# Groups 3 to 5 of a decayed-attention and SwiGLU kernel take the row-pair layout (NAT0 from 3 to 6)

## The chip, the core and the metric

The kernel runs on one core of one Trainium2 chip. The metric is the device time of one execution in microseconds (us). Five engines take part: TensorE (PE, matrix multiplies), VectorE (DVE), ScalarE (ACT), GpSimd (POOL) and SyncE (SP, which here only issues transfers). Each engine works through its own list of instructions in order and waits at an instruction until the data, the buffer and the bank it needs are there. Transfers (DMAs) are issued by SP and by ACT and run on 16 shared DMA engines.

## The reference

Inputs are q, k and v of shape 4 batches x 8 heads x 768 rows x 64, one decay `lam` a head (0.97 to 0.99), and three weight matrices. Attention goes over blocks of 64 rows and carries a 64x64 state a head:

```python
intra = np.einsum('bhic,bhjc->bhij', qb, kb) * Dmask[None]     # lam ** (i - j) below the diagonal
intra = np.einsum('bhij,bhjd->bhid', intra, vb)
inter = np.einsum('bhid,bhde->bhie', qb * lam_pow[None], kv_state)
out[:, :, sl] = intra + inter
kv_state = lam_block * kv_state + np.einsum('bhsd,bhse->bhde', kb_dec, vb)
```

The result, as a matrix x of 3072 x 512, goes through a gated block: `(silu(x @ w_gate) * (x @ w_val)) @ w_out`, with an inner width of 1536. Everything is float32 outside; the kernel computes in bf16 with float32 sums.

## The kernel before

**Tiling.** The rows are cut into 12 groups: a group is 256 rows of one batch, all 8 heads. Groups 0 to 3 are the first 256 rows of batches 0 to 3, groups 4 to 7 the second 256, groups 8 to 11 the last. Two groups make one tile of 512 tokens for the gated block, so there are six tiles, t = 0 to 5. All the work is written out by hand in one order: `steps` lists the gated block's 12 column steps of each tile (`ffn_fc`, lines 516 to 535), and `plan` hangs other work after chosen steps (`at(...)`, lines 669 to 748). The scheduling of the framework is manual: on each engine instructions stand in the order in which they are written.

**A group's path.** `load_group` (L244) issues its loads on SP. `cast_scaled` (L258, groups 3 and up) casts k to bf16 on ACT (L261), multiplies q by the decay on DVE (L263), then calls `dma_transpose` (L251), which puts one transposing DMA on SP (L254), and then `load_group(g + 2)`: SP issues the loads of the group after next behind the transpose. `v_scale` (L236) multiplies v by the decay on POOL. On PE come `upd_mm` (L386, products k x v for the state), `scores` (k x q), `inter` (L469, state x q) and `intra` (L482, masked scores x v). The scores are masked on DVE from PSUM into `ssb`; the copies of `upd_mm`'s result out of PSUM (`ups`, L410) and the casts of the outcome (`evac`, L494) are ACT's, in a few places DVE's; `state` (L416) adds up the state on POOL.

**Two layouts.** `NAT0` (L56) says how many groups take the first one.

- g < NAT0, the row-pair layout: a partition holds two adjacent rows of a head. One DMA loads all of k (or q, or v) of a group (L99), in pieces of 512 bytes. The group is handled as two halves of 128 rows. `scores` issues 32 products of 64x128 into four banks and defers four masks of 128x512 (L330, L337); `intra` is 32 products of 64x128; `inter` is 8 (first group of a batch) or 16 products of 64x128. `state` adds two parts.
- g >= NAT0, the plain layout: a partition holds rows p and p + 128, and half of the partitions hold the heads in reverse. k and q of a group take four DMAs each, v two (L106), in pieces of 256 bytes. The group is handled as four quarters of 64 rows. `scores_n` (L344) issues 32 products of 64x64 into two banks and defers two masks (L356, L361); `intra` is 32 products of 64x64; `inter` is 24 or 32 of 64x64; `state` adds four parts and casts three partial states in between (L427, L436, L438).

Masks are deferred in the list `later`; `run_later` works off one or two of them after each step. `attend(g)` (L558) holds `inter` of g, the update of g + 1, the scores of g + 1 and `intra` of g; for g + 1 >= NAT0 the scores stand before `intra`, else behind it (L564, L568).

**What orders the work around the change.** SP's list from the output weights on is, before: six loads of output weights (L228), ten loads of group 3, ten of group 4, the transpose of group 3, ten loads of group 5, the transpose of group 4, ten of group 6, the transpose of group 5, ten of group 7, the transpose of group 6, and so on. All DMAs of SP and ACT share eight completion semaphores in turn, and each waits until the one before it on its semaphore has landed. PSUM is used as a ring of eight banks (`bank`, L79): `ring` counts up and each new result takes the next one.

PE's order there is: the last steps of tile 0, the first half of tile 1 (s1a), `ffn_out` of tile 0 (three blocks of 12 products of 128x512, L546), `ahead(3)` (update, state and scores of group 3), the fourth block, s1a steps 9 and 10, `core(3)`, step 11, the second half s1b with `ahead(4)` after its step 5, `ffn_out(1, 0)`, `attend(4)`, three more blocks of `ffn_out`, `attend(5)`, and from there tile 2.

Of the kernel before, what the change touches and what calls it, by code (L numbers as in the profile page):

```python
# [14 lines left out]
def bap(t: bass.AP, ap_dims, extra_offset=0) -> bass.AP:  # L15
    return bass.AP(tensor=t.tensor, offset=t.offset + extra_offset,
                   ap=[list(t.ap[0])] + [list(d) for d in ap_dims])


@with_exitstack  # L20
def kernel(
    ctx: ExitStack,
    tc: tile.TileContext,
    q: bass.AP,
    k: bass.AP,
    v: bass.AP,
    lam: bass.AP,
    moe_w_gate: bass.AP,
    moe_w_val: bass.AP,
    moe_w_out: bass.AP,  # L30
    out: bass.AP,
):
    nc = tc.nc
    with tc.manual_schedule():
        _body(ctx, tc, nc, q, k, v, lam, moe_w_gate, moe_w_val, moe_w_out, out)


def _body(ctx, tc, nc, q, k, v, lam, moe_w_gate, moe_w_val, moe_w_out, out):
# [14 lines left out]

    NAT0 = 3  # L56
    NB = 4
    PB = B // 2
    groups = [(t % PB * 2 + j, t // PB) for t in range(NG // 2) for j in range(2)]
# [25 lines left out]
    def gsrc(t, g, h0):  # L85
        b, i = groups[g]
        return bass.AP(tensor=t.tensor,
                       offset=t.offset + b * H * S * D + i * 2 * BLK * D + h0 * S * D,
                       ap=[[2 * D, 2 * M], [S * D, H - h0], [1, 2 * D]])
# [3 lines left out]
    def load_fp32(g, eng, src, what, h0=0, h1=H):  # L93
# [3 lines left out]
        t = st[(what, g)]  # L97
        if g < NAT0:
            eng.dma_start(out=t[:, h0:h1], in_=gsrc(src, g, h0)[:, 0:h1 - h0])  # L99
# [87 lines left out]
    def vfac(g, h0, h1):  # L187
        return bap(dec, [[8, h1 - h0], [1, 2], [0, D]], 8 * h0 + (0 if g < NAT0 else 4))

    def qfac(g):  # L190
        return bap(dec, [[8, H], [1, 2], [0, D]], 2) if g < NAT0 else bap(qdn, [[2, H], [1, 2], [0, D]])

# [119 lines left out]
    def scores(g, cs=(0, 1), warm=0):  # L312
        if g >= NAT0:
            scores_n(g)
            return
        tt = st[("qkt", g)]
        sp = {(c, h2): bank() for c in cs for h2 in range(2)}
        warm_into(sp[(cs[0], 0)], warm)
        if ("ssb", g) not in st:
            st[("ssb", g)] = ssb_pool.tile([128, 2, HP, 2, BLK], BF16, name="ssb", tag="ssb")  # L320
        ssb = st[("ssb", g)]
        for c in cs:
            for hi in range(2):
                for s in range(2):
                    for b2 in range(2):
                        for h2 in range(2):
                            hp = 2 * c + hi
                            dp = slice(h2 * 64, h2 * 64 + 64)
                            n = (hi * 2 + s) * BLK
                            nc.tensor.matmul(  # L330
                                sp[(c, h2)][b2 * M:b2 * M + M, n:n + BLK],
                                tt[dp, 0, s, hp, b2 * M:b2 * M + M],
                                tt[dp, 1, :, hp, b2 * M:b2 * M + M],
                                start=True, stop=True, skip_group_check=True)
            for h2 in range(2):
                def do_mask(c=c, h2=h2):
                    nc.vector.tensor_tensor(  # L337
                        out=ssb[:, h2, 2 * c:2 * c + 2].rearrange("p a s n -> p a (s n)"),
                        in0=sp[(c, h2)].rearrange("p (a x) -> p a x", a=2),
                        in1=bap(causal, [[0, 2], [1, 2 * BLK]]),  # L340
                        op=ALU.mult)
                later.append(do_mask)

    def scores_n(g):  # L344
        tt = st[("qkt", g)]
        sp = [bank() for _ in range(2)]
        ssb = ssb_pool.tile([128, 2, HP, 2, BLK], BF16, name="ssb", tag="ssb").rearrange(
            "p a h s n -> p (a h s n)")[:, 0:2 * BLK * H // 2].rearrange("p (a h n) -> p a h n", a=2, h=H)
        st[("ssb", g)] = ssb
        for hp in range(HP):  # L350
            for s in range(2):
                for h2 in range(2):
                    for r in range(2):
                        row, hq = (1 - h2, HP - 1 - hp) if r else (h2, hp)
                        dp, rm = slice(row * 64, row * 64 + 64), slice(r * M, r * M + M)
                        nc.tensor.matmul(sp[h2][rm, (hp * 2 + s) * M:(hp * 2 + s) * M + M],  # L356
                                         tt[dp, 0, s, hq, rm], tt[dp, 1, s, hq, rm],
                                         start=True, stop=True, skip_group_check=True)
        for h2 in range(2):
            def do_mask(h2=h2):  # L360
                nc.vector.tensor_tensor(out=ssb[:, h2], in0=sp[h2].rearrange("p (a x) -> p a x", x=M),  # L361
                                        in1=bap(causaln, [[0, 2 * HP], [1, M]]), op=ALU.mult)
            later.append(do_mask)
# [6 lines left out]
    def upd_mm(g, up=None):  # L370
# [4 lines left out]
        for s in range(2):  # L375
            for hp in range(HP):
                for r in range(2):
                    if g >= NAT0 and i == NG // B - 1 and 2 * s + r == 3:
                        continue
                    for h2 in range(2):  # L380
                        ps = slice(r * M, r * M + M)
                        h = 2 * hp + h2
                        if g >= NAT0 and r:
                            h = H - 1 - h
# [405 lines left out]
```

## Time and profile before

| what | value |
|---|---|
| median of 3 runs | 245.96 us (245.46 to 246.36) |
| the profiled execution's own time | 246.36 us |
| its span, first to last instruction | 244.6 us |
| mean granted PE clock | 0.965 of full |
| PE busy | 223.0 us, 91% |
| ACT, POOL, DVE busy | 108.4, 95.4, 88.1 us |
| the chain that ended last | PE 76%, DMA 13%, POOL 6% |
| SP's queue (q1) | 93026 packets, 32.65 MB |
| packets under 512 bytes, of all | 76418 of 97565 |

PE's own work fills nine tenths of the span, so this kernel is PE's length plus PE's pauses. The chain says who stretches it beyond that: 13% of the chain is DMA. The shares of busy time of the other engines (36 to 44%) say nothing of a bound. The lines to look for are those in which PE stands idle, and the granted clock behind each of them.

### The profile page before, as it was taken

The page shows a single profiled execution, that of the slowest core. Times are in us where ns is not written, and L with a number is a line of the kernel's source. Part 1 is how long each engine was busy: PE and PEld are TensorE (multiplying, and loading weights), DVE is VectorE, ACT ScalarE, POOL GpSimd, SP SyncE. Part 2 cuts the span into 40 slices and gives each one's busy share as a digit, 9 for nine tenths or more (in the row PEclk, how much of TensorE's full clock was granted, in tenths as well). Part 3 has the DMA queues.
Part 4 walks back from the last instruction along what each step waited for, and adds up shares of the span by engine and source line. Part 5 has one row for each costly group of instructions (what it writes and reads, how often), then busy time and mean ns, then how long its engine had stood idle before and what let it go on. Part 6 is the DMA issues. An engine that isn't in the chain of part 4 may idle for free.

```text
span 244.6 us, 6085 instructions
## 1 busy us (share of the span) xinstructions
PE 223.0 (91%) x2497; PEld 122.3 (50%) x2508; DVE 88.1 (36%) x151; ACT 108.4 (44%) x211; POOL 95.4 (39%) x146
## 2 busy tenths in 40 slices
PE   7999998993499979379999999999999999999994
PEld 3665456841258844165545445454454444444443
DVE  3663356420316640035564426235324222242200
ACT  5876764734026543224646327235362352222211
POOL 5566647333700778770495607409124000000000
PEclk9999999999579999958999999999999999999999
DMA  7999999699896957977888874410510111001122
GB/s 210 345 362 372 360 351 354 144 240 251 182 244 156 219 138 181 200 168 179 181 183 192 191 182 120 129 46 3 129 46 3 43 46 43 30 15 43 43 86 86
DMA packets 97565, 39.71 MB, mean 162 GB/s; under 512 B 76418, under 2 KB 93058, under 8 KB 97538
## 3 DMA queue, kind: packets, MB, share of 16 engines
q1 hardware_dynamic: 93026, 32.65, 53.5%
q10 hardware_dynamic: 4512, 6.69, 7.5%
q8 instruction: 19, 0.31, 0.5%
q14 instruction: 8, 0.07, 0.1%
HBM read 28.31 MB, written 6.29 MB: 141 GB/s over the span
## 4 chain that ended last, share of the span: by engine, by line
PE 76%; DMA 13%; POOL 6%; ACT 1%; issue 1%; DVE 1%; SPq 0%; POOLq 0%; DVEq 0%; ACTq 0%
PE bank L546 24%; PE bank L524 22%; PE bank L531 21%; DMA qkt<-qk 7%; DMA wraw<-in_moe_w_val_dram 3%; DMA v<-in_v_dram 3%; PE bank L482 2%; POOL v_s L239 2%; POOL kvf L427 1%; PE bank L386 1%; PE bank L469 1%; PE bank L356 1%; PE bank L168 1%; PE bank L293 1%; POOL kvs L430 1%
## 5 line engine op out<-in xcount | busy, mean ns | idle before, releaser
L534 DVE TENSOR_TENSOR h<-sil,bank 128x512 bf16<-128x512 bf16 (+1 forms) x89 | 51.9, 585 | 103.8 <-PE bank L531 87.4
L524 PE MATMUL bank<-xt,wg_sb 128*128 128x512 bf16 (+1 forms) x356 | 78.6, 344 | 0.0
L531 PE MATMUL bank<-xt,wv_sb 128*128 128x512 bf16 (+1 forms) x356 | 78.2, 343 | 0.0
L528 ACT ACTIVATE sil<-bank 128x512 bf16<-128x512 f32 (+1 forms) x89 | 46.1, 520 | 47.6 <-PE bank L524 43.8
L546 PE MATMUL bank<-wo_sb,h 128*128 128x512 bf16 (+1 forms) x289 | 66.3, 380 | 0.7 <-issue 0.2
L531 PEld LDWEIGHTS <-wv_sb 128*128 128x128 bf16 x356 | 35.5, 100 | 28.1
L524 PEld LDWEIGHTS <-wg_sb 128*128 128x128 bf16 x356 | 34.2, 100 | 27.4 <-issue 0.5
L546 PEld LDWEIGHTS <-h 128*128 128x128 bf16 x300 | 29.7, 100 | 33.8 <-issue 2.7
L548 ACT COPY osb<-bank 128x512 f32<-128x512 f32 (+1 forms) x24 | 13.9, 577 | 62.8 <-PE bank L546 62.8
L427 POOL TENSOR_TENSOR kvf<-kvs,ups 128x256 f32<-128x256 f32 x8 | 5.8, 726 | 57.4 <-ACT ups L410 54.7
L239 POOL TENSOR_TENSOR v_s<-v,dec 128x1024 bf16<-128x1024 f32 (+1 forms) x14 | 23.5, 1683 | 9.9 <-DMA v<-in_v_dram 9.7
L361 DVE TENSOR_TENSOR ssb<-bank,causaln 128x512 bf16<-128x512 f32 x18 | 12.2, 687 | 32.7 <-PE bank L356 32.6
L436 POOL CAST kvn<-kvf 64x256 bf16<-64x256 f32 x34 | 16.6, 487 | 2.1
L427 POOL TENSOR_TENSOR kvf<-kvf,ups 128x256 f32<-128x256 f32 x22 | 16.8, 764 | 1.1
L356 PE MATMUL bank<-qkt 64*64 64x64 bf16 x288 | 4.9, 206 | 12.2 <-DMA qkt<-qk 12.2
L494 ACT CAST xt<-bank 128x512 bf16<-128x512 f32 x21 | 12.1, 632 | 7.3 <-PE bank L482 6.9
L410 ACT COPY ups<-bank 128x512 f32<-128x512 f32 (+1 forms) x24 | 10.8, 503 | 3.0 <-PE bank L386 2.1
L263 DVE TENSOR_TENSOR qk<-qraw,qdn 128x1024 bf16<-128x1024 f32 x9 | 11.1, 1230 | 0.3 <-DMA qraw<-in_q_dram 0.3
L356 PEld LDWEIGHTS <-qkt 64*64 64x64 bf16 x288 | 3.9, 114 | 12.4 <-DMA qkt<-qk 12.4
L261 ACT CAST qk<-kraw 128x1024 bf16<-128x1024 f32 x9 | 9.4, 1039 | 0.0
L222 POOL CAST wv_sb<-wraw 128x1024 bf16<-128x1024 f32 (+1 forms) x7 | 6.4, 920 | 6.9 <-DMA wraw<-in_moe_w_val_dram 6.8
L337 DVE TENSOR_TENSOR ssb<-bank,causal 128x512 bf16<-128x512 f32 x12 | 7.9, 682 | 1.6 <-PE bank L330 1.6
(61 smaller groups left out, 116.2 us busy)
## 6 DMA issues: line engine op xcount, KB each, us to landing
out_dram<-osb ACTq DMA_DIRECT2D x23, 256.0 KB, 2.4
v<-in_v_dram SPq DMA_DIRECT2D x22, 256.0 KB, 4.2
kraw<-in_k_dram SPq DMA_DIRECT2D x36, 128.0 KB, 3.1
qraw<-in_q_dram SPq DMA_DIRECT2D x36, 128.0 KB, 3.2
woraw<-in_moe_w_out_dram SPq DMA_DIRECT2D x6, 512.0 KB, 9.3
wraw<-in_moe_w_gate_dram SPq DMA_DIRECT2D x5, 512.0 KB, 7.3
wraw<-in_moe_w_val_dram SPq DMA_DIRECT2D x5, 512.0 KB, 6.9
kraw<-in_k_dram SPq DMA_DIRECT2D x4, 256.0 KB, 4.4
```

The lines of the kernel that those rows point to most:

```text
L239: eng.tensor_tensor(out=st[("vs", g)][:, h0:h1], in0=st[("v", g)][:, h0:h1].rearrange("p h (s d) -> p h s d", s=2), in1=vfac(g, h0, h1), o ...
L356: nc.tensor.matmul(sp[h2][rm, (hp * 2 + s) * M:(hp * 2 + s) * M + M], tt[dp, 0, s, hq, rm], tt[dp, 1, s, hq, rm], start=True, stop=True, s ...
L361: nc.vector.tensor_tensor(out=ssb[:, h2], in0=sp[h2].rearrange("p (a x) -> p a x", x=M), in1=bap(causaln, [[0, 2 * HP], [1, M]]), op=ALU.mult)
L427: nc.gpsimd.tensor_tensor(out=o, in0=f, in1=u, op=ALU.add)
L436: nc.gpsimd.tensor_copy(out=o[64 - h2 * 64:128 - h2 * 64], in_=f[h2 * 64:h2 * 64 + 64])
L494: fns[r](out=xt[:, g % 2, :, r].rearrange("p h (m s) -> p h s m", s=2) if g < NAT0 else xt[:, g % 2, :, :, r * M:r * M + M], in_=op[r].rea ...
L524: nc.tensor.matmul(gp[:, 0:N], wg_sb[:, mc, fs], xt[:, b0 // 2:b1 // 2, mc].rearrange("p g b n -> p g (b n)"), start=(mc == 0), stop=(mc = ...
L528: nc.scalar.activation(sil[:, 0:N], gp[:, 0:N], AF.Silu)
L531: nc.tensor.matmul(vp[:, 0:N], wv_sb[:, mc, fs], xt[:, b0 // 2:b1 // 2, mc].rearrange("p g b n -> p g (b n)"), start=(mc == 0), stop=(mc = ...
L534: nc.vector.tensor_tensor(out=h_sb[:, fc, b0:b1].rearrange("p b n -> p (b n)"), in0=sil[:, 0:N], in1=vp[:, 0:N], op=ALU.mult)
L546: nc.tensor.matmul(ps, h_sb[:, fc, b], wo_sb[:, fc, c0:c1], start=(fc == 0), stop=(fc == FC - 1))
L548: fn(out=osb[:, c0:c1], in_=ps)
```

## The change

One constant is changed:

```diff
-    NAT0 = 3
+    NAT0 = 6
```

Groups 3, 4 and 5 then take the row-pair layout wherever the code asks `g < NAT0` or `g >= NAT0`. They keep `cast_scaled` with its transposing DMA. On the engines' lists this does the following.

- SP: the ten loads of each of groups 3, 4 and 5 become three (k, q, v whole, L99), 512-byte pieces in place of 256-byte ones. The order of loads and transposes stays; the loads of groups 6 and up stay ten.
- PE: `scores` (L330) in place of `scores_n` (L356) for groups 3 to 5; products of 64x128 in place of 64x64 in `intra` and `inter`, with 8 in place of 24 in `inter` of group 3 and 16 in place of 32 in groups 4 and 5. In `attend(4)` the scores of group 5 now stand behind `intra` of group 4.
- DVE: four masks (L337) in place of two (L361) for each of the three groups. L263 reads its factor from `dec` in place of `qdn`.
- ACT: `ups` copies of 256 columns in place of 512; for group 3 one cast more (`kvn`, L402).
- POOL: for group 3 one add, one multiply and one cast in place of three adds, five casts, one multiply and one cast; for groups 4 and 5 two adds, one cast of a partial state, one multiply and one cast in place of four adds, five casts of partial states, one multiply and one cast.
- PSUM: `scores` takes four banks of the ring in place of two, so that the banks that follow shift by two for each of the three groups.
- The eight DMA semaphores are dealt out anew, since there are fewer DMAs.

## The prediction

> **What bounds the kernel now.** I read the page's chain first: PE 76%, DMA 13%, POOL 6%. So the end is set by PE and by what PE waits for. Next came the waits of PE between 38 and 106 us, which add up to nearly all of its idle time behind 38 us; from 110 us to the end the same view shows 0.3 us of waits. Each row gives what was waited for: us in total, times, longest.
>
> ```profile
> PE bank L356 <- DMA qkt<-qk: 12.2, 2, 7.0
> PE bank L386 <- POOL v_s L239: 1.8, 2, 1.6
> ```
>
> The reader is to see two long waits for a transposed group (qkt) and one for a scaled v. PE's timeline puts them in place (start, duration, instruction, idle time before it):
>
> ```profile
> 56.92 0.45 PE L386 MATMUL bank<-v_s,qk 64*64 64x64 bf16 x32
> 64.39 0.64 PE L356 MATMUL bank<-qkt 64*64 64x64 bf16 x32 [7.03 <-DMA qkt<-qk]
> 90.02 0.45 PE L386 MATMUL bank<-v_s,qk 64*64 64x64 bf16 x32 [1.55 <-POOL v_s L239]
> 105.20 0.64 PE L356 MATMUL bank<-qkt 64*64 64x64 bf16 x32 [5.16 <-DMA qkt<-qk]
> ```
>
> These are the scores of group 3, the update of group 5 and the scores of group 6. Behind the two long pauses PE is slow as well. The stages (window, length, busy us of PE, PEld, DVE, ACT, POOL, then the granted clock, DMA share, GB/s):
>
> ```profile
> 64.40:70.30 5.90, 5.68 (x45) 2.48 (x47) 2.42 (x3) 0.00 (x0) 1.95 (x2) 0.50 0.87 197
> 88.40:90.10 1.70, 0.15 (x19) 0.08 (x12) 0.00 (x0) 0.47 (x2) 1.57 (x1) 1.00 0.59 185
> 105.20:111.30 6.10, 6.10 (x88) 4.56 (x89) 2.13 (x4) 2.35 (x6) 3.71 (x5) 0.50 0.72 162
> ```
>
> After 7.03 and 5.16 us of idleness the clock was 0.50 for about 6 us; after 1.55 us it stayed 1.00. Last, why the transposes are late: SP's timeline.
>
> ```profile
> 48.47 3.35 SPq L106 DMA_DIRECT2D kraw<-in_k_dram  x4
> 51.92 3.31 SPq L106 DMA_DIRECT2D qraw<-in_q_dram  x4
> 55.46 1.41 SPq L106 DMA_DIRECT2D v<-in_v_dram  x2
> 57.06 4.49 SPq L254 DMA_TRANSPOSE qkt<-qk  x1
> ...
> 90.75 3.13 SPq L106 DMA_DIRECT2D qraw<-in_q_dram  x4
> 93.98 1.19 SPq L106 DMA_DIRECT2D v<-in_v_dram  x2
> 95.34 4.82 SPq L254 DMA_TRANSPOSE qkt<-qk  x1
> ```
>
> DVE finished the cast of group 3 at 51.28 (50.06 + 1.22), but SP was issuing loads of group 4 until 56.87, so the transpose left at 57.06 and landed 7.3 us later. Group 6 is alike: cast done at 87.17, transpose at 95.34, behind the ten loads of group 7, landing 9.8 us later. **The bound between 57 and 111 us is SP's list of issues**, 10 loads a group at some 0.63 us each.
>
> **What goes.**
>
> - First pause: 7.03. Its slow clock: the scores took 0.64 where group 4's took 0.40 (79.69 to 80.09), and twelve products of L546 took 65.03 to 70.27 = 5.24 where later blocks of twelve take 2.59. That is 0.24 + 2.65 = 2.9.
> - The wait for v_s of group 5: 1.55.
> - Second pause: 5.16. Its slow clock: 105.20 to 111.30 holds scores, intra and six groups of four 256-column products, at full clock 0.40 + 0.37 + 6 x 0.44 = 3.4, so 2.7.
> - Sum 19.3 us.
>
> **First pause, step by step.** In the new list SP has six issues for groups 3 and 4 in place of twenty. The new form's rows are the loads of group 2 (1.23, 2.54 and 0.69 us of issue). Six times 0.7 to 2.5 from 35.33 gives 40 to 50; the wait on the weight transfers ahead of them (their semaphores come round again, the last seen at about 45) is inside that. So SP is free before the cast ends at 51.0 to 51.3, and the transpose leaves then. It lands in 3.8 (fastest row, nothing beside it) to 7.3 us: 55 to 58.5, and PE asks at 57.36. I take no pause; at the upper end 1.1 us are left, short enough to keep the clock by the 1.55 row.
>
> Bytes could still hold it: groups 3 and 4 are 3.1 MB behind the output weights. From 6 to 9 us, where k, q and v of the first groups ran in 512-byte pieces, the DMA view shows 345 GB/s; a stretch of 256-byte pieces, 72 to 73 us, shows 290. At 345 the backlog that starts at about 44 is gone by 53, and the transpose lands by 57.
>
> **A rule against it.** The Trainium skill, DMA: Bandwidth & Descriptors, section "Issuing engines are not separate DMA queues", says that the time a sequencer takes to start a DMA is usually small beside the DMA itself. By that rule fewer issues would buy next to nothing and the sum would be a loss of about 2 us. The rows agree for a single load (0.63 against 3.1 to landing), but twenty in one line held back a transpose for 5.8 us.
>
> **Wait for v_s of group 5.** POOL ran the state of group 4 from 80.63 to 88.06, then v_s for 1.91. Two adds at 0.72, a cast at 0.40, a multiply at 0.61 and a cast at 0.40 make 2.9 in place of 7.4: 4.5 earlier covers 1.55. This goes.
>
> **Second pause.** Everything behind 57.4 moves 9.9 us earlier, and asks earlier too, by 1.55 more; so the transpose of group 6 has to gain on PE. SP, new: transpose 4 when its q is cast, at about 61.3 (scores at 57.4, three masks of 0.69, one cast of 1.22; free since some 58). It holds SP to 63 or 64.4 (1.6 to 3.1 in the rows). Ten loads of group 6 at 0.63 take it to 70 or 71. Transpose 5, whose cast is done at 68.9, leaves at 70.8 and holds SP to 74.2. Ten loads of group 7 take it to 80.6. In the old run two loads between 82 and 112 us waited 6.3 us in all for an output transfer with the same semaphore (87.14 to 90.75, among group 7's, is the larger part); in the new list no load of group 7 follows an output on its semaphore that isn't long done. Transpose 6 leaves at 80.7 and lands 5.5 to 9.8 later: 86.2 to 90.5.
>
> PE asks for it at: 57.4 + (88.47 - 64.39 = 24.1) - 2.9 + 1.2 (below) = 79.8 for the end of inter of group 4; update and intra 0.9; scores of group 5 0.6; three output blocks 7.8 and 0.3 (below); inter and update 0.8: about 90.2. So it lands at the latest as it is asked for. The same holds on the way: transpose 4 lands by 67.4, asked at 70.2; transpose 5 by 77.5, asked at 80.7. **I take the second pause as gone**, with 1.0 us left here or at the scores of group 7, whose transpose comes behind the loads of group 8.
>
> **What comes.**
>
> - PE: scores 34.44 to 35.01 against 0.40 (+0.17), intra 39.68 to 40.26 against 72.80 to 73.17 (+0.21). Inter of 16 x 64x128 isn't in the trace; between 8 of them (0.41) and 32 of 64x64 (about 0.43 to 0.5), I take no change. Three groups: 1.1.
> - DVE: six masks of 0.68, 4.1 us. Behind scores 3 an output block (2.59) and behind scores 5 three of them cover. Behind scores 4 there are only steps of 0.87, and the ring comes round after four allocations to the score banks: with masks and h products in turn, masks 3 and 4 end at about 3.4 and 4.4 us from the scores' start, where PE asks at 3.2 and 3.7. Cost 0.75; if masks are early 0, if all four are waited for 2.7.
> - ffn_out(1, 1) takes the first bank of group 4's outcome, which ACT casts last: 0.3.
> - The factor of L263 read from `dec`: not in the trace; between the plain DVE cast (0.42 for half, 0.85) and POOL's product with `dec` (1.91), near its own row, 1.22. Off the path either way.
> - Fewer copies on ACT and POOL: off the path, nothing.
>
> Sum: 19.3 - 1.1 - 0.75 - 0.3 - 1.0 = 16.2. The profiled execution took 246.36 (span 244.6 and 1.76 around it), so 230.2; it stands 0.4 above the median, so **229.8 us**.
>
> **Rivals.**
>
> A. The second pause stays. The transpose of group 6 still stands behind ten loads in the old form, and one landed in 9.8. If each such load takes 0.84 (as group 4's ten did, 48.47 to 56.87 with their gaps) instead of 0.63, transpose 6 leaves at 85 and lands at 95: 5 us of pause and the 2.7 of clock come back in place of the 1.0: 229.8 + 6.7 = 236.5. Whether a smaller rest costs the clock isn't in the trace between 1.55 and 5.16. Chance 0.20. (The skill, TensorE: Matmul & The Clock Gate, section "What's actually happening", puts the fall at about 3.4 us of idleness; by it a rest of under 3.4 stays without the 2.7.)
>
> B. The first pause only shrinks, since the transposes themselves are slow under load (7.3), and the weight casts or the loads come later by a few us: half of the first pause and all of the second: 239 to 243. Chance 0.06.
>
> C. Slower. The pacing goes: six large loads stand in front of transpose 3 in the DMA queues instead of in SP's list. If these pieces moved at the 225 GB/s that the stretch 47 to 57 shows, 3.1 MB from 44 would end at 58, the transpose would land where it did, 64.4, and each later one likewise; the added PE work and mask waits (2.1) would remain: 248. It decides from about 240 GB/s downward. Against it stand the 345. Chance 0.06.
>
> No measurable change (within 0.3%, 0.7 us, about what a measurement here can tell from none): 0.02.
>
> Forecast 0.66. Low end: all 19.3 and half of the added PE work, 227; high end rival A, 237. **Faster 0.92, same 0.02, slower 0.06.**
>
> **What would show it.** Right: SP's transpose of group 3 at 51 to 52, no wait over 1.5 us at L330 at about 57, clock 1.00 from 57 to 80, POOL's state of group 4 about 3 us long, scores of group 6 at 90 to 92. Wrong: a wait for qkt at the scores of group 3 (B, C), a pause over 3 us at group 6's (A), DVE late by more than 1 us behind scores 4.

## The result and the profile after

| | before | after |
|---|---|---|
| median of 4 runs | 245.71 us (242.93 to 246.36) | 232.24 us (231.17 to 234.25) |
| the profiled execution | 246.36 us, span 244.6 | 234.25 us, span 232.5 |
| granted clock, mean | 0.965 | 1.000 |

The ratio is 0.948, with a 95% interval of 0.938 to 0.959: 13.5 us less, where 16.2 were forecast (229.8 us, range 227 to 237). A few executions of the kernels below run slow as a whole at a lower granted clock (one of e6 at 286.77 us, one of e10 at 243.69), and the ratios leave them out.

PE's waits from 38 us to the end, after the change (total us, times, longest):

```profile
PE bank L356 <- DMA qkt<-qk: 3.6, 2, 2.9
PE bank L330 <- DMA qkt<-qk: 1.3, 1, 1.3
PE bank L482 <- ACT guard L451: 1.2, 4, 0.4
```

Where 12.2 us were spent waiting for transposes, 4.9 are left, and POOL's v_s is no longer in the list. PE's timeline tells which they are:

```profile
57.86 0.64 PE L330 MATMUL bank<-qkt 64*64 64x128 bf16 x32 [1.32 <-DMA qkt<-qk]
...
75.47 0.60 PE L531 MATMUL bank<-xt,wv_sb 128*128 128x256 bf16 x4 [0.33 <-DVE ssb L337]
...
83.12 7.93 PE L546 MATMUL bank<-wo_sb,h 128*128 128x512 bf16 x35 [0.39 <-ACT xt L494]
...
92.61 0.45 PE L356 MATMUL bank<-qkt 64*64 64x64 bf16 x32 [0.74 <-DMA qkt<-qk]
...
106.03 0.45 PE L356 MATMUL bank<-qkt 64*64 64x64 bf16 x32 [2.87 <-DMA qkt<-qk]
```

The scores of group 3 wait 1.32 in place of 7.03, those of group 6 0.74 in place of 5.16, and a new pause of 2.87 stands at the scores of group 7. Behind scores 4 one wait of 0.33 for a mask is listed, and `ffn_out(1, 1)` waits 0.39 for its bank. The stages behind the first two (the columns are those of the prediction's stages, the clock stands behind the five engines):

```profile
57.80:63.50 5.70, 5.37 (x67) 3.39 (x69) 5.18 (x6) 2.76 (x7) 3.61 (x4) 1.00 1.00 322
92.60:97.10 4.50, 4.49 (x96) 3.85 (x97) 2.62 (x6) 3.66 (x8) 3.80 (x8) 1.00 0.58 151
```

Where the clock was 0.50 it is 1.00 now. SP's timeline:

```profile
43.23 2.15 SPq L99 DMA_DIRECT2D kraw<-in_k_dram  x1
45.47 1.35 SPq L99 DMA_DIRECT2D qraw<-in_q_dram  x1
46.87 1.44 SPq L99 DMA_DIRECT2D v<-in_v_dram  x1
51.53 3.19 SPq L254 DMA_TRANSPOSE qkt<-qk  x1
...
84.71 3.67 SPq L254 DMA_TRANSPOSE qkt<-qk  x1
88.42 7.04 SPq L106 DMA_DIRECT2D kraw<-in_k_dram  x4
95.51 2.67 SPq L106 DMA_DIRECT2D qraw<-in_q_dram  x4
98.28 1.20 SPq L106 DMA_DIRECT2D v<-in_v_dram  x2
99.64 4.21 SPq L254 DMA_TRANSPOSE qkt<-qk  x1
```

Group 4's loads end at 48.31 in place of 56.87, and the transpose of group 3 leaves when its cast is done. The one of group 6 leaves at 84.71 in place of 95.34. Behind it the loads of group 8 are still in the old form, and the transpose of group 7 stands behind them. SP's waits put 3.3 us of the 7.04 for group 8's k down to an output transfer that had the same completion semaphore.

### The profile page after: what moved, and what is told of

Same layout as the page of the kernel before. It is cut to its first block, busy times and chain, and to the rows that moved or that the text cites. A ratio compares the mean times of both kernels' runs of the same rounds, so it can differ in the third digit from the quotient of the medians.

```text
span 232.5 us, 5937 instructions
## 1 busy us (share of the span) xinstructions
PE 219.2 (94%) x2449; PEld 120.5 (52%) x2460; DVE 95.4 (41%) x157; ACT 108.0 (46%) x212; POOL 84.9 (36%) x127
## 4 chain that ended last, share of the span: by engine, by line
PE 81%; DMA 11%; DVE 3%; SPq 1%; ACT 1%; issue 1%; ACTq 0%; DVEq 0%
PE bank L524 26%; PE bank L531 26%; PE bank L546 22%; DMA qkt<-qk 9%; PE bank L482 2%; DMA qraw<-in_q_dram 2%; DVE ssb L337 2%; PE bank L469 1%; SPq L99 1%; PE bank L330 1%; PE bank L356 1%; PE bank L386 1%; PE bank L293 1%; DVE h L534 0%; PE bank L168 0%
## 5 line engine op out<-in xcount | busy, mean ns | idle before, releaser
L524 PE MATMUL bank<-xt,wg_sb 128*128 128x512 bf16 (+1 forms) x356 | 77.0, 339 | 0.0
L546 PE MATMUL bank<-wo_sb,h 128*128 128x512 bf16 (+1 forms) x289 | 63.9, 370 | 1.0 <-ACT xt L494 0.4
L548 ACT COPY osb<-bank 128x512 f32<-128x512 f32 (+1 forms) x24 | 13.9, 577 | 55.8 <-PE bank L546 55.8
L337 DVE TENSOR_TENSOR ssb<-bank,causal 128x512 bf16<-128x512 f32 x24 | 15.6, 683 | 11.7 <-PE bank L330 11.6
L361 DVE TENSOR_TENSOR ssb<-bank,causaln 128x512 bf16<-128x512 f32 x12 | 8.2, 687 | 12.2 <-PE bank L356 12.0
L436 POOL CAST kvn<-kvf 64x256 bf16<-64x256 f32 x24 | 12.5, 521 | 1.5
L427 POOL TENSOR_TENSOR kvf<-kvf,ups 128x256 f32<-128x256 f32 x16 | 11.6, 725 | 0.6
L410 ACT COPY ups<-bank 128x256 f32<-128x256 f32 (+1 forms) x24 | 9.5, 449 | 1.1 <-PE bank L386 0.7
L482 PE MATMUL bank<-ssb,v_s 64*64 64x128 bf16 (+1 forms) x384 | 7.3, 207 | 1.7 <-ACT guard L451 1.2
L263 DVE TENSOR_TENSOR qk<-qraw,qdn 128x1024 bf16<-128x1024 f32 x6 | 8.6, 1432 | 0.0
L482 PEld LDWEIGHTS <-v_s 64*64 64x64 bf16 x384 | 5.8, 105 | 3.0 <-issue 3.0
```

The costliest lines, as they stand in the source:

```text
L337: nc.vector.tensor_tensor(out=ssb[:, h2, 2 * c:2 * c + 2].rearrange("p a s n -> p a (s n)"), in0=sp[(c, h2)].rearrange("p (a x) -> p a x", ...
L427: nc.gpsimd.tensor_tensor(out=o, in0=f, in1=u, op=ALU.add)
L436: nc.gpsimd.tensor_copy(out=o[64 - h2 * 64:128 - h2 * 64], in_=f[h2 * 64:h2 * 64 + 64])
L482: nc.tensor.matmul(op[r][h2 * 64:h2 * 64 + 64, cols(g, hp, s)], v_s[ps, 2 * hp + h2, s], ssb[ps, h2, hp * 2 + s] if g >= NAT0 else ssb[ps, ...
L524: nc.tensor.matmul(gp[:, 0:N], wg_sb[:, mc, fs], xt[:, b0 // 2:b1 // 2, mc].rearrange("p g b n -> p g (b n)"), start=(mc == 0), stop=(mc = ...
L546: nc.tensor.matmul(ps, h_sb[:, fc, b], wo_sb[:, fc, c0:c1], start=(fc == 0), stop=(fc == FC - 1))
```

## The experiments

Three theories stood against each other. S: SP's list ahead of each transpose was shortened, by fewer issues. B: the larger pieces move faster. P: the rest of the layout does it, POOL's shorter state above all. Edits add lines, so a line number in a view can differ from the one named before by a few. Medians below are beside the kernel before on the same chip: 244.27 us for e1 to e5, 244.79 for c0, e9, e7 and e6, 244.14 for e10 and e11.

**e1: ten issues again, 512-byte pieces.**

```diff
-            eng.dma_start(out=t[:, h0:h1], in_=gsrc(src, g, h0)[:, 0:h1 - h0])
+            n = (h1 - h0) if g < 3 else 4 if what == "v" else 2
+            for a in range(h0, h1, n):
+                eng.dma_start(out=t[:, a:a + n], in_=gsrc(src, g, a)[:, 0:n])
```

> The changed kernel (NAT0 = 6) with the loads of groups 3 to 5 cut by heads into ten issues a group again, still in 512-byte pieces; nothing else differs. Theory S (SP's list of issues is what was shortened): the transpose of group 3 leaves behind twenty issues again, at 55 to 57 us in place of 51.5, both long pauses of PE come back with the half clock behind them, and the time is 241 to 247. Theory B (the larger pieces make the transfers faster): the pieces are those of the changed kernel, so 231 to 235. Theory P (the shorter chain of states on POOL, and the layout otherwise): likewise 231 to 235.

Measured: 233.86 us, ratio 0.957 (0.951 to 0.963). S, which had 241 to 247, fails in this form; B and P had 231 to 235. SP's timeline for group 4 and the transpose of group 3 shows why:

```profile
44.97 1.99 SPq L101 DMA_DIRECT2D kraw<-in_k_dram  x4
47.06 1.96 SPq L101 DMA_DIRECT2D qraw<-in_q_dram  x4
49.06 1.02 SPq L101 DMA_DIRECT2D v<-in_v_dram  x2
50.83 3.51 SPq L256 DMA_TRANSPOSE qkt<-qk  x1
```

The same ten issues take 5.1 us (44.97 to 50.08) in place of 8.4: as long as the three of the changed kernel (43.23 to 48.31). The transpose leaves early, but it lands some 9 us later: the scores of group 3 start at 59.81, behind a pause of 3.23. Why it lands so late is open.

**e2: the transpose of group 3 amid the loads of group 4.**

```diff
-    at(s0[7], load_group, 4)
+    at(s0[7], load_group, 4, "k")
...
         dma_transpose(g)
+        if g == 3:
+            load_group(4, "qv")
```

> The kernel before, layout and loads as they were, with the transpose of group 3 moved up in SP's list: it stands behind the four k loads of group 4 and ahead of group 4's q and v loads. Theory S: the transpose leaves at about 52 in place of 57.06 and the first pause of PE shrinks from 7.03 us to under 1.5. The list is no shorter, so each later transpose gains only what the first did: 52 + 38 (as from 57.06 to 95.34) puts that of group 6 at 90, and pauses of 3 to 6 us in all come back at the scores of groups 4 to 6; 237 to 242. Theories B and P: nothing that they name is changed, 244 to 247.

Measured: 240.80 us, ratio 0.987 (0.982 to 0.993), inside S's range and under that of B and P. The transpose left at 50.82 and the first pause went. PE's timeline shows where it came back:

```profile
73.36 0.45 PE L358 MATMUL bank<-qkt 64*64 64x64 bf16 x32 [2.25 <-DMA qkt<-qk]
84.77 0.44 PE L358 MATMUL bank<-qkt 64*64 64x64 bf16 x32 [0.66 <-DMA qkt<-qk]
100.42 0.64 PE L358 MATMUL bank<-qkt 64*64 64x64 bf16 x32 [6.35 <-DMA qkt<-qk]
```

The pauses add up to 9.3 us, where S had 3 to 6. So SP's list is the bound over several groups: an earlier place helps one transpose, and only a shorter list helps those behind it.

**e3: plain layout, three issues of 256-byte pieces.**

```diff
+        if g < 6:
+            eng.dma_start(out=t.rearrange("p h (s d) -> p (h s) d", s=2),
+                          in_=bass.AP(tensor=src.tensor, offset=base,
+                                      ap=[[D, 128], [S * D // 2, 2 * H], [1, D]]))
+            return
```

> The kernel before, plain layout with all its work on PE, DVE, ACT and POOL, where k, q and v of groups 3 to 5 are each loaded by one issue of 2048 pieces of 256 bytes. The rows that arrive are not the right ones for half of the partitions and columns, so the output is not the reference's; the amount of data and of work is the same. Theory S: ten issues a group become three, the first pause goes and the second goes or shrinks to under 3 us, 231 to 236 (the wait of 1.55 for v_s may stay, the added PE work of the other layout is not there). Theory B: pieces of 256 bytes as before, 244 to 247. Theory P: POOL's chain as before, 244 to 247. If one issue of 2048 pieces holds SP as long as four of 512, S fails in its form and the number of pieces would be the bound: 244 to 247 with issues of some 2.5 us each.

Measured: 235.06 us, ratio 0.961 (0.956 to 0.967). That is S's range (231 to 236) and not that of B and P (244 to 247): without larger pieces, fewer issues bring most of the gain too. SP's timeline:

```profile
45.06 2.19 SPq L104 DMA_DIRECT2D kraw<-in_k_dram  x1
47.35 2.51 SPq L104 DMA_DIRECT2D qraw<-in_q_dram  x1
49.91 2.32 SPq L104 DMA_DIRECT2D v<-in_v_dram  x1
52.41 4.61 SPq L259 DMA_TRANSPOSE qkt<-qk  x1
```

And PE's:

```profile
59.29 0.45 PE L361 MATMUL bank<-qkt 64*64 64x64 bf16 x32 [2.60 <-DMA qkt<-qk]
...
95.96 0.44 PE L361 MATMUL bank<-qkt 64*64 64x64 bf16 x32 [2.19 <-DMA qkt<-qk]
```

Each issue of 2048 small pieces holds SP for 2.2 to 2.5 us, 7.2 for the group: little shorter than ten (8.4). Over groups 3 and 4 together the list falls from 21.5 us (35.33 to 56.87) to 18.0 (34.23 to 52.23). The pauses are down to 2.60 and 2.19. The second has a cause of its own: the list ahead of the transpose of group 6 was done at 84.37, but the transpose left at 90.23, and SP's waits put 5.7 us of this down to an output transfer with the same semaphore. Behind the first pause the clock still fell, to 0.50 from 60.6 to 63.8; behind the second it stayed. The fall shows in twelve products of 128x512, beside those of e1, whose pause was longer:

```profile
60.38 2.76 PE L548 MATMUL bank<-wo_sb,h 128*128 128x512 bf16 x12
```

```profile
59.67 4.45 PE L551 MATMUL bank<-wo_sb,h 128*128 128x512 bf16 x12
```

The first row is e1's, behind 3.23 us of pause, the second e3's, behind 2.60. So 1.7 of the 2.9 us that the prediction put behind the first pause is still paid here, and the 2.7 behind the second is not.

**e5: NAT0 = 9.** The edit is the constant alone.

> NAT0 = 9: groups 6 to 8 take the row-pair layout too. Theory S: in the changed kernel the next pause is that of 2.9 us at the scores of group 7, whose transpose stands behind ten loads of group 8 (four of them took 7.04 us); with three loads a group for 6 to 8 it leaves as soon as its cast is done, that pause and the 0.74 at group 6 go, against 3 x 0.4 us more of PE work and some waits for masks: 229 to 232. Theory P expects a gain from POOL's shorter states, which nothing waits for there: no change from 232, or 1 us more for the PE work.

Measured: 233.04 us, ratio 0.954 (0.950 to 0.958): no better than NAT0 = 6, and above S's 229 to 232. No wait for a transpose is left; what PE waits for is the row-pair layout's own:

```profile
PE bank L482 <- ACT guard L451: 1.7, 5, 0.5
PE bank L524 <- ACT xt L494: 1.2, 3, 0.4
PE bank L531 <- DVE ssb L337: 0.7, 2, 0.3
```

With the larger products (0.4 a group by the prediction's estimate) this takes back about what the pauses had cost.

**e9: plain layout, ten issues of 512-byte pieces.** The edit is e1's, in the branch of the plain layout, for g < 6.

> The kernel before, plain layout with all its work on the engines, ten issues a group for groups 3 to 5 as before, but each in 512-byte pieces (by heads, the row-pair source). The rows land in the wrong places for the plain layout, so the output is not the reference's; data and work are the same in amount. Theory S2, formed after the run with ten issues in the changed layout: SP is held by what the DMA engines and the queue take for the pieces, 8.4 us for a group in ten issues of 256-byte pieces, 5.1 in ten of 512-byte pieces, 7.1 in three of 256-byte pieces. By it the transpose of group 3 leaves within 1 us of its cast, the first pause is under 4 us and keeps the clock, and the time is 232 to 237. Theory P (POOL's chain and the layout made the gain in that run): 243 to 247. Theory S in its first form (the count of issues): 243 to 247.

Measured: 233.82 us, ratio 0.959 (0.951 to 0.967). Count of issues, products, masks and POOL's chain are as before. The pieces changed, and with them an issue of k or q reaches 128 partitions in place of 64, which isn't separated. All but some 1.5 us of the gain is there, and the intervals overlap. So the gain doesn't need P, nor the smaller count of S; the second form, S2, holds. The list of groups 3 and 4 takes 15.5 us here (34.23 to 49.73).

**c0: the changed kernel again.**

> The changed kernel as it is, beside the three that follow: all theories 231 to 233.5. Its profile tells whether the pause of 2.9 us at the scores of group 7 and the long casts of q (2.52 and 2.97 in place of 1.22 us) come again.

Measured: 232.26 us. In its profile (span 229.8) the casts of q take 1.25 and 1.45, the transpose of group 3 leaves at 50.64, nothing waits at its scores, and the scores of group 7 wait 1.76.

**e7: v of group 3 scaled on DVE** (`v_scale, 3, nc.vector`).

> The changed kernel with v of group 3 scaled on DVE, behind the cast of q of group 3, in place of POOL. Theory L (the cast of q and POOL's scaling, both reading two or one operands from SBUF, shut each other out; the cast waited for POOL's instruction of 1.91 us to end): the cast of group 3 takes 1.22 us in place of 2.52, the transpose of group 3 leaves about 1.3 us earlier, the pause of 1.32 at the scores of group 3 goes, the cast of group 4 stays long (2.9) beside POOL's scaling of group 4; 230 to 232. Rival (the cast is slower because its factor is read from the other table, with a wider step): the cast of group 3 stays at 2.5 and nothing is gained, 231.5 to 233.5.

Measured: 233.11 us against c0's 232.26: no gain. The cast of group 3 took 1.22, as theory L says, with the same table; but c0 had no pause there to win. In its profile the clock fell to 0.50 behind a pause of 1.95 at the scores of group 7, where c0's stayed at full behind 1.76.

**e6: v loads one transpose later.**

```diff
         dma_transpose(g)
-        load_group(g + 2)
+        if g < 4:
+            load_group(g + 2)
+        else:
+            if g > 4:
+                load_group(g + 1, "v")
+            load_group(g + 2, "kq")
```

> The changed kernel with the v loads of groups 6 and up issued one transpose later: behind the transpose of the group before theirs, so that only eight loads stand ahead of each transpose from that of group 5 on. Theory S2: 1.2 us less of SP's list and 0.5 MB less in the queues ahead of each transpose; the transpose of group 7 is issued when its cast ends, the pause of 2.9 us at the scores of group 7 falls to under 1.5, and that of 0.74 at group 6 goes: 229.5 to 232. Rival (that pause comes from loads of k that wait for an output transfer with the same semaphore, whatever the length of the list): no change, 231.5 to 233.5.

Measured: 229.41 us, ratio 0.940 (0.933 to 0.948), against c0's 232.26 beside it: the fastest kernel of the study, a tenth of a microsecond under S2's range. PE's waits from 38 us on hold no transpose any more:

```profile
PE bank L487 <- ACT guard L456: 1.4, 5, 0.5
PE bank L551 <- ACT xt L499: 0.4, 1, 0.4
PE bank L536 <- DVE ssb L342: 0.3, 1, 0.3
```

The transpose of group 7 left at 96.11, when its cast was done (95.97); in the changed kernel it left 1.6 us after its cast, in c0 1.2. That is S2's forecast. The rival isn't ruled out by it: a new order deals the semaphores anew, and SP's waits for output transfers among the loads of that stretch fell too, from 3.3 us in the changed kernel and 3.9 in c0 to 2.4.

**e10 and e11: the same move of v with NAT0 = 3 and with NAT0 = 5.**

> The kernel before (NAT0 = 3, 256-byte pieces), its only edit that v of each group from 4 on is loaded one transpose later, so that eight loads stand ahead of each transpose in place of ten. Theory S2: the transpose of group 3 leaves about 1.5 us earlier (55.5 on the old run's clock, 54 to 55 where the start is a little faster), which leaves 3.5 to 5 us of the first pause, and each group's list is 1.2 us shorter: the one of group 6 leaves about 5 us earlier. 236 to 242. If the layout is needed for the gain: 243 to 246.

> NAT0 = 5 with v loaded one transpose later (from group 6 on, as in the fastest kernel so far with NAT0 = 6): group 5 goes back to the plain layout, with ten loads of 256-byte pieces, two masks less and smaller products. Theory S2: eight fewer pieces' worth of list matter little there, since the transpose of group 5 had 2 to 4 us to spare; 0.4 us less of PE work, 228.5 to 231. Rival (each group that stays with 256-byte pieces costs a third of the gain of 13 us): 232 to 235.

Measured: e10 237.33 us, ratio 0.972 (0.968 to 0.977), pauses of 2.62 and 2.52 left, with the clock at 0.50 for some 3.5 us behind both; the move alone gives half of the change's gain. Its list ended at 53.00 and the cast of group 3 at 50.36, but the transpose left at 55.41: SP's waits put 2.3 us down to an output transfer with the same semaphore. e11 231.07 us, ratio 0.947 (0.943 to 0.951), at the edge of S2's range and under the rival's; its transpose of group 6 left at 86.32, where e6's left at 80.65. Its cast was done at 77.65 and its list at 82.93; here SP waited 3.2 us for an output transfer.

So beside the length of the list there is a second thing that holds a transpose back: the output transfer that happens to have its semaphore (5.7 us in e3, 2.3 in e10, 3.2 in e11). No run changes the semaphores alone.

## Why the prediction was right, and where it wasn't

- **Right: which waits go.** Both long pauses, the slow clock behind them and the wait for v_s went. The transpose of group 3 left at 51.53 (forecast 51.0 to 51.3). That this time fits is luck: the cast started 1.2 us earlier than before (48.85 against 50.06) and took 1.3 longer. POOL's state of group 4 took 3.0 us, 71.89 to 74.91 (2.9).
- **Right in kind, wrong in its reason: "SP's list of issues, 10 loads a group at some 0.63 us each".** That SP's list is the bound stands by e2 and e10, and e6 agrees. That the count of issues alone makes its length doesn't: for group 4, ten issues of 512-byte pieces take 5.1 us, ten of 256-byte pieces 8.4, three of 256-byte pieces 7.2, three of 512-byte pieces 5.1. For groups 3 and 4 together it is 21.5 before, 18.0 with fewer issues alone (e3), 15.5 with larger pieces alone (e9) and 13.9 with both (34.43 to 48.31). The size of the pieces moved the list more than the count did, and either alone is enough for most of the gain. Whether the DMA engines or the making of the pieces' descriptors sets these times isn't separated here. A hint: from 46 to 48 us the DMA share was 0.84 before (189 GB/s), 1.12 in e3 (254 GB/s) and 0.98 in e9 (275 GB/s).
- **The rule that was set against the change** said that the number of issues counts for little. Between 512-byte forms that is so: e1's ten against three is 233.86 against 232.24, with intervals that overlap. With 256-byte pieces it isn't: e3's three against ten is 235.06 against 244.27. The prediction set the rule aside for a reason that covers half of the case. The Trainium skill, DMA: Bandwidth & Descriptors, section "Specifications", gives 512 bytes as the least transfer for full rate; e9 is the run that shows what that is worth here.
- **"The factor of L263 ... near its own row, 1.22. Off the path either way" failed.** In the profiled execution the casts of groups 3 and 4 took 2.52 and 2.97. This made the transpose of group 4 leave at 63.24 (forecast 61.3). At group 3 it is the likely cause of the 1.32 that is left of the first pause, since a cast of 1.22 would have let the transpose go 1.3 earlier; no run shows it, as e7 had no pause there to win.
- **Mis-sized: the 1.0 for a rest at group 6 or 7.** It measured 0.74 + 2.87 in the profiled execution, 1.76 in c0. The 2.87 kept the clock by luck: behind 1.94 (e11) and 1.95 (e7) at the same place it fell. Group 6's transpose left at 84.71, not 80.7: 1.9 from the cast of group 4, the rest from a transpose that held SP 4.14 and loads of group 7 that took 7.6 us, not 6.4. PE asked later too, so that the pause stayed small.
- **Sized right:** the masks behind scores 4. One wait of 0.33 is listed, but the eight steps behind the scores took 4.19 us (71.72 to 75.91) where they took 3.50 before (80.09 to 83.59): 0.7 for 0.75. The bank of `ffn_out(1, 1)` took 0.39 for 0.3.
- **Rivals.** C's mechanism, the backlog of bytes ahead of the transpose, shows in e3, where the pieces stay small: group 4's issues end at 52.23 and the transpose lands 6.9 us after it leaves, which leaves 2.60 of the pause and not all of it. The reading isn't firm, since in e1 the transpose lands some 9 us after it leaves, behind larger pieces. A's mechanism came one group later than it was placed: group 8's loads took 11.1 us (88.42 to 99.48), 3.3 of them a wait for an output transfer, and the pause behind was 2.87, without the clock. For group 7 the prediction had looked for such a wait and rightly found none; for group 8 it had not looked. B's half pause stayed out in c0 and left 1.32 in the other profile.

The profiled execution took 234.25 where the sum gave 230.2, 4.05 more, and its PE was 0.8 ahead of the old run at 56 us: 4.9 to account for. The rest of the first pause is 1.3, the pauses at groups 6 and 7 are 2.6 above the 1.0, the masks of group 3, behind the long cast, held PE for 0.3, and the guards took some 0.4 more than before: 4.6. Some 0.3 us stays without a name.

## What to carry to other kernels

A transfer that others wait for has a place in the list of the engine that issues it: read when its operands were ready and when it left, and count what stands between. Shorten that list by larger contiguous pieces first, then by fewer issues, and move out of it what is needed later (e6: v behind the next transpose). Look also at which output transfer shares a completion semaphore with the transfer that others wait for. A pause can cost more than its length, since the clock can fall behind it: in these runs from 1.94 us on, but not each time. With both pauses cut to less than half, e3 has some 70% of this gain.

## What the runs showed of the hardware that was not expected

**POOL's scaling holds up DVE's cast.** The cast of q on DVE (L263) reads two operands from SBUF. The changed kernel, the scaling of v on POOL and the cast beside it:

```profile
48.38 1.91 POOL L239 TENSOR_TENSOR v_s<-v,dec 128x1024 bf16<-128x1024 f32 x1 [4.14 <-DMA v<-in_v_dram]
60.10 1.91 POOL L239 TENSOR_TENSOR v_s<-v,dec 128x1024 bf16<-128x1024 f32 x1
```

```profile
48.85 2.52 DVE L263 TENSOR_TENSOR qk<-qraw,dec 128x1024 bf16<-128x1024 f32 x1
...
60.13 2.97 DVE L263 TENSOR_TENSOR qk<-qraw,dec 128x1024 bf16<-128x1024 f32 x1
```

Both casts end 1.1 us after POOL's instruction does (50.29 and 62.01): DVE stood for 1.3 and 1.75. In e9, with the other table, it is the same:

```profile
47.81 1.91 POOL L244 TENSOR_TENSOR v_s<-v,dec 128x1024 bf16<-128x1024 f32 x1 [3.63 <-DMA v<-in_v_dram]
```

```profile
48.87 1.94 DVE L268 TENSOR_TENSOR qk<-qraw,qdn 128x1024 bf16<-128x1024 f32 x1
```

With POOL away the cast takes 1.22 (e7, either table). So it isn't the table. The Trainium skill, SBUF — State Buffer, section "Who interferes with whom", says that a DVE instruction with two SBUF inputs contends with a GpSimd instruction that reads SBUF; these rows agree. Before the change v of group 3 landed after the cast, and they didn't meet: the faster loads brought the collision.

**The clock.** The length of a pause alone doesn't say whether the clock falls. It stayed at 1.00 behind 2.19 (e3), 2.87 (the changed kernel) and 3.23 us (e1), and it fell to 0.50 behind 1.94 (e11), 1.95 (e7), 2.25 (e2), 2.52 and 2.62 (e10), 2.60 (e3) and 5.16 (before). Behind the pauses under 3 us the fall came 0.2 to 1.2 us after PE had gone on, and lasted some 3.5 us. Between 1.55 and 5.16 the prediction had left this open; the 3.4 that it quotes as a limit isn't one in these runs. What else decides is open.

**Issues.** One issue of 512 KB in 512-byte pieces holds SP for 0.54 us as the first behind a transpose (k of group 5 in the changed kernel) and 1.4 right behind other loads; the same in 256-byte pieces 0.53 and 2.2 to 2.5 (e3).
